# Two token blocks of a gated MoE layer through seven of eight block products, with transposes moved to TensorE

## The chip, the cores and the metric

The program runs on one core of a Trainium2 chip. The metric is the device time of one execution in microseconds (us), the median over the runs shown. The profile is one execution, recorded by the hardware profiler. Engines: TensorE (PE, with its weight loads as PEld), VectorE (DVE), ScalarE (ACT), GpSimd (POOL) and SyncE (SP, which here only issues DMAs).

## What is computed

Three layers in a row, all in fp32 at the interface:

```
h    = x @ omega.T - |x|^2/2 ; phi(x) = exp(h - max(h)) / sqrt(128)        (x = q or k, scaled)
attn = phi(q) @ (phi(k).T @ v) / (phi(q) @ sum(phi(k)) + 1e-6)             4 x 8 heads, 576 x 64
y    = (sigmoid(attn @ w_gate) * (attn @ w_val)) @ w_out                   2304 tokens, 512 -> 1536 -> 512
out  = soft mixture of 8 experts over y (dispatch and combine softmax, 4 slots each, 512 -> 1024 -> 512)
```

## The kernel before, in words

The 32 heads are handled as 16 attention units of two heads (`step_chunks`, L701). A unit's numerators (`chunk_num`, L658) yield a piece of x, the MoE input with features on partitions; x is split into a rounded part (hi) and a rest (lo), and stays in SBUF as tile `XT` of its block (`xt`, L696). The 2304 tokens are five blocks: four of 512 and one of 256 (`BLOCKS`, L27).

The MoE layer runs in 60 steps (`STEPS`, L33), a step being one block j and one slice f of 128 of the 1536 hidden features. A step has a gate product (`gate`, L828), a value product (`val`, L839) and an output product (`down`, L853). Each is four products of 128x128 weights, and each of those three TensorE passes (`three`, L452: hi times hi, hi times lo, lo times hi), so 12 instructions. In blocks 0 to 3 they are 128x512, in block 4 128x256. The weights come from DRAM scratch `wscr` (`load_w`, L750) and are split into hi and lo for every step (`split_w`, L798: hi on ACT or DVE, lo on POOL or DVE). The gate's sigmoid is made of Abs, Exp, Ln and Exp on ACT with one DVE instruction between, so that ACT keeps one activation table for the whole program.

The blocks stand in this order (`GROUPS`, L32): block 0's first six slices, block 1, block 0's rest, blocks 2, 3 and 4. Attention units 0 to 7 go with the first group, 8 to 11 with block 1, 12 to 15 with block 2. For units 10 and later (`N_SPLIT`, L58) the phi(q) tiles are transposed not on TensorE but by 32x32 DVE transposes and a round trip through DRAM (`turn_q`, L642: eight DVE transposes, 2 DMAs out and 8 in for a unit). The last layer's logits, transposes and slot sums follow each block (`moe2_chunks`, L967); its weights w1 are loaded through ACT's queue (`load_w1`, L984) into tiles that have come free (`EXTAGS`, L973), w2 through SP's queue.

What order each engine gets is settled when the program is built: every instruction is recorded with a due time (from `SPAN`, L75, and the job list at the end of `body`) and the engines that may run it, and `schedule` (L240) lists them by due time, dependence and a table of costs (`cost`, L200). On the chip each engine runs its list in order, and waits only on semaphores. PSUM has eight banks: `ga` and `va` for the gate and value products, `o0` to `o3` for the output sums, two of `fl` for everything else.

Of the kernel before, what the change touches and what calls it, by code (L numbers as in the profile page):

```python
# [34 lines left out]
ENDS = {i for i, (j, f) in enumerate(STEPS) if (j, f) in {(j, e - 1) for j, _, e in GROUPS}}  # L35
DONE = [1, 0, 2, 3, 4]
# [21 lines left out]
N_SPLIT = 10  # L58
N_NUM = 10
LATE8 = 0.3  # L60
# [14 lines left out]
SPAN = [88.0, 115.0, 60.0, 120.0, 105.0, 45.0]  # L75
# [11 lines left out]
HOP = 0.16  # L87
TURN = 0.2
# [15 lines left out]
class Plan:  # L104
# [135 lines left out]
    def schedule(self):  # L240
# [46 lines left out]
        dma = 0.0  # L287
        order = []
# [60 lines left out]
        while ev:  # L349
# [13 lines left out]
            for e in E:  # L363
                while free_at[e] <= now + 1e-9:
# [21 lines left out]
                    c, held = self.cost(e, alt[1], alt[3], outs, ins)  # L386
                    if held:
                        port = now + c
# [31 lines left out]
def body(ctx, tc, nc, qkT, tok, von, omT, wall, phi, w1, w2, ident_d, srep_d, rrep_d, mask_d, out):  # L420
# [31 lines left out]
    def three(ps, lhs, rhs, first=True, last=True):  # L452
        (lh, ll), (rh, rl) = lhs, rhs
        PE.matmul(ps, lh, rh, start=first, stop=False)
        PE.matmul(ps, lh, rl, start=False, stop=False)
        PE.matmul(ps, ll, rh, start=False, stop=last)
# [86 lines left out]
    def prep_qk(u, kind):  # L543
# [3 lines left out]
        if u == N_SPLIT and kind == 0:  # L547
            split_regions()
# [109 lines left out]
    def chunk_num(u, half):  # L658
# [13 lines left out]
        else:  # L672
# [77 lines left out]
    def load_w(i):  # L750
# [47 lines left out]
    def split_w(i, part):  # L798
        if i >= NB * NF:
            return  # L800
        end = (i, part) == (NB * NF - 1, 2)
# [5 lines left out]
        if (i, part) == (LAST - 1, 2):  # L807
            load_part(5)
# [613 lines left out]
```

## Time and profile before

| | |
|---|---|
| median of 3 runs | 677.5 us (676.54 to 678.06) |
| span of the profiled execution | 676.7 us; the page gives no time beyond it |
| TensorE busy, instructions | 652.3 us, 4292 |
| VectorE busy | 446.8 us |
| ScalarE busy | 430.3 us |
| GpSimd busy | 276.9 us |
| DMA moved | 144.78 MB, mean 214 GB/s |

Busy time counts the union of an engine's instructions; matmuls overlap each other, so that one lasts longer than the distance from its start to the next one's. A row of the timeline merges instructions of one kind: start, time from the first start to the last end, engine, line, instruction, output and inputs by tile name, sizes, count, and in brackets how long the engine was idle before and what ended that.

### The profile page before, as it was taken

How to read it: one execution, taken by the hardware profiler on the slowest of the kernel's cores; microseconds unless marked ns; L12 is line 12 of the kernel's file. 1: busy time of each engine (PE TensorE's matmuls, PEld its weight loads, DVE VectorE, ACT ScalarE, POOL GpSimd, SP SyncE). 2: the span in 40 equal slices, each digit the busy share in tenths (PEclk: the TensorE clock that was granted, in tenths of full speed). 3: DMA queues.
4: the chain of work that ended last, by engine and by line, in shares of the span. 5: the costliest groups of instructions: out<-in, count | busy, mean ns of one | idle time of the engine just before them, and what ended most of it. 6: DMA issues, size and time to landing. Idle time of an engine off the chain costs nothing. (4 is left out here: it accounts for less than half of the span.)

```text
span 676.7 us, 12729 instructions
## 1 busy us (share of the span) xinstructions
PE 652.3 (96%) x4292; PEld 521.2 (77%) x4292; DVE 446.8 (66%) x1399; ACT 430.3 (64%) x971; POOL 276.9 (41%) x240
## 2 busy tenths in 40 slices
PE   7898999999999999899999999999999999999994
PEld 5675777768788888788788888777888789889663
DVE  4888989889987474766686666556543337666322
ACT  5898989889787575767567666546344445664011
POOL 0546335454455344445344444343544444342100
PEclk9999999999999999999999999999999999999998
DMA  7887857677875337575557424579963339767997
GB/s 256 294 268 235 286 187 261 216 235 264 294 235 191 89 124 222 182 201 161 164 166 227 133 67 136 166 234 349 257 223 93 99 104 312 220 226 256 352 348 221
DMA packets 64241, 144.78 MB, mean 214 GB/s; under 512 B 7600, under 2 KB 21680, under 8 KB 64176
## 3 DMA queue, kind: packets, MB, share of 16 engines
q1 hardware_dynamic: 58352, 126.60, 58.2%
q10 hardware_dynamic: 5824, 17.37, 7.7%
q8 instruction: 34, 0.56, 0.3%
q14 instruction: 31, 0.25, 0.1%
HBM read 122.44 MB, written 17.30 MB: 206 GB/s over the span
## 5 line engine op out<-in xcount | busy, mean ns | idle before, releaser
L413 POOL TENSOR_TENSOR w<-ws,w 128x512 fp32r<-128x512 f32 x139 | 181.4, 1307 | 247.4 <-ACT w L413 88.4
L413 PE MATMUL ga<-XT,w 128*128 128x512 f32 (+1 forms) x720 | 170.3, 377 | 2.3 <-POOL XT L413 1.2
L413 PE MATMUL va<-XT,w 128*128 128x512 f32 (+1 forms) x720 | 167.4, 375 | 0.9 <-DVE ga_a L413 0.6
L413 PE MATMUL o<-gt,w 128*128 128x512 f32 (+1 forms) x720 | 166.6, 374 | 0.9 <-POOL w L413 0.9
L413 PEld LDWEIGHTS ga<-XT,w 128*128 128x128 f32 x720 | 123.7, 188 | 29.8 <-issue 3.5
L413 PEld LDWEIGHTS o<-gt,w 128*128 128x128 f32 x720 | 124.8, 188 | 26.1 <-issue 2.2
L413 PEld LDWEIGHTS va<-XT,w 128*128 128x128 f32 x720 | 123.8, 189 | 27.3 <-issue 3.2
L413 ACT ACTIVATE w<-ws 128x512 fp32r<-128x512 f32 x110 | 69.1, 628 | 59.6 <-POOL w L413 17.2
L413 ACT ACTIVATE g<-g 128x128 f32<-128x128 f32 (+5 forms) x213 | 78.2, 420 | 23.2 <-DVE g L413 12.3
L413 PE MATMUL fl<-g,g 64*128 64x128 f32 (+4 forms) x686 | 83.1, 313 | 3.6 <-ACT g L413 1.7
L413 PEld LDWEIGHTS fl<-g,g 64*128 64x128 f32 (+2 forms) x686 | 59.8, 182 | 24.3 <-issue 9.0
L413 ACT ACTIVATE ga_a<-ga_a 128x512 f32<-128x512 f32 (+1 forms) x120 | 69.8, 582 | 12.8 <-DVE ga_a L413 10.9
L413 ACT ACTIVATE ga_a<-ga 128x512 f32<-128x512 f32 (+1 forms) x60 | 33.1, 552 | 63.4 <-PE ga L413 63.0
L413 DVE SCALAR_TENSOR_TENSOR ga_a<-ga,ga_a 128x512 f32<-128x512 f32 (+1 forms) x60 | 38.0, 633 | 36.9 <-ACT ga_a L413 36.0
L413 DVE CAST w<-ws 128x512 fp32r<-128x512 f32 x52 | 22.5, 432 | 52.9 <-PE ga L413 34.7
L413 DVE TENSOR_TENSOR ga_a<-va,ga_a 128x512 f32<-128x512 f32 (+1 forms) x60 | 38.0, 634 | 24.2 <-ACT ga_a L413 16.7
L413 ACT ACTIVATE x2T<-g 128x512 f32<-128x512 f32 x72 | 46.0, 664 | 5.1 <-DVE x L413 3.0
L413 ACT ACTIVATE g1b<-g1b,g 128x128 f32<-128x128 f32 x128 | 41.1, 390 | 7.1 <-DVE g L413 7.1
L413 ACT ACTIVATE ga_a<-ga_a,one_b 128x512 f32<-128x512 f32 (+1 forms) x60 | 40.6, 677 | 1.2
L413 DVE CUSTOM_DVE_ANT_0 g<-fl,g 128x128 f32<-128x128 f32 x142 | 32.4, 286 | 9.0 <-PE fl L413 8.7
L413 DVE TENSOR_SCALAR x2T<-x2T 128x512 f32<-128x512 f32 (+1 forms) x72 | 35.9, 515 | 2.0 <-ACT x2T L413 1.8
L413 POOL TENSOR_TENSOR g<-g 128x640 f32<-128x640 f32 (+1 forms) x18 | 22.2, 1231 | 34.2 <-DMA g<-in_tok 24.7
(202 smaller groups left out, 773.6 us busy)
## 6 DMA issues: line engine op xcount, KB each, us to landing
ws<-wscr SPq DMA_DIRECT2D x42, 512.0 KB, 3.8
ws<-wscr SPq DMA_DIRECT2D x78, 256.0 KB, 3.2
g<-in_wall SPq DMA_DIRECT2D x36, 512.0 KB, 5.0
wscr<-x SPq DMA_DIRECT2D x36, 256.0 KB, 4.6
g<-in_qkT SPq DMA_DIRECT2D x15, 576.0 KB, 4.8
g<-in_tok SPq DMA_DIRECT2D x15, 576.0 KB, 4.9
g<-in_w ACTq DMA_DIRECT2D x16, 512.0 KB, 5.5
XT<-in_w ACTq DMA_DIRECT2D x12, 512.0 KB, 5.5
```

Source lines behind the costliest of these rows:

```text
L413: ins = getattr(self.eng[e], method)(*a, **k)
```

## The change

Blocks 2 and 3 leave `STEPS` and become a pair. For two slices f and f+1 at once, the gate stage (and the value stage) of the pair is a product of 2x2 blocks: 256 hidden features by 512 inputs, by 512 inputs times 1024 tokens. It is now computed by seven block products in place of eight (Strassen's scheme in the form with 15 sums). A block product is six TensorE instructions of 128x512 (`product` in `pair_up`). The sums of tokens are made once (`pair_tokens`), those of weights for each pair of slices and each of the two stages (`pair_split`), and those of results at each evacuation (`pair_up`). All eight attention units 8 to 15 now stand beside block 1 and the rest of block 0. `chunk_num` writes x of blocks 2 and 3 unsplit in fp32 (`xq`). The output products of block 2 follow each pair of slices, those of block 3 come in a stage of their own after it, from gated values kept in SBUF (`GB`); w_out is split once for each of the two. In the pair and in block 4 the gate is one Sigmoid, whose activation table has to be loaded, and Exp's again where Exp follows. `N_SPLIT` of 16 leaves all transposes on TensorE. The w1 loads have other tiles and due times (`EXTAGS`).

```diff
-GROUPS = [(0, 0, CUT), (1, 0, NF), (0, CUT, NF), (2, 0, NF), (3, 0, NF), (4, 0, NF)]
+GROUPS = [(0, 0, CUT), (1, 0, NF), (0, CUT, NF), (4, 0, NF)]
+PAIR = (2, 3)
-N_SPLIT = 10
+N_SPLIT = 16
...
-SPAN = [88.0, 115.0, 60.0, 120.0, 105.0, 45.0]
+SPAN = [88.0, 143.0, 71.0, 45.0]
+SPANQ = 147.0
+SPAND = 33.0
...
         a = T([128, 512], "ga_a", F32, 2)[:, 0:n]
+        if i >= LAST:
+            ACT.activation(out=a, in_=ps, func=AF.Sigmoid)
+            return a
...
+    def pair_tokens():
+
+        a, b = (xq(j) for j in PAIR)
+        b11, b21, b12, b22 = a[:, 0:2], a[:, 2:4], b[:, 0:2], b[:, 2:4]
...
+        for k, r in zip((6, 5, 7, 3, 4, 2, 1), regs):
+            OT[k] = r
+        sum_of(t1, b12, b11, ALU.subtract)
+        hi_lo(OT[1], b11)
+        hi_lo(OT[5], t1)
+        hi_lo(OT[2], b21)
+        sum_of(t2, b22, t1, ALU.subtract, ("DVE",))
+        hi_lo(OT[6], t2, ("DVE",))
+        sum_of(t3, b22, b12, ALU.subtract, ("DVE",))
+        hi_lo(OT[7], t3)
+        sum_of(b21, b21, t2, ALU.subtract)
+        hi_lo(OT[4], b21)
+        hi_lo(OT[3], b22)
...
+    def pair_split(part):
+
+        x, y = WR[:, 2 * part, :], WR[:, 2 * part + 1, :]
+        a11, a12, a21, a22 = x[:, 0:256], x[:, 256:512], y[:, 0:256], y[:, 256:512]
+        s1, s2 = SG[7][:, 0:256], SG[7][:, 256:512]
+        sum_of(s1, a21, a22, ALU.add)
+        sum_of(s2, s1, a11, ALU.subtract)
+        hi_lo(OW[6], s2)
+        hi_lo(OW[1], a11)
+        sum_of(a21, a11, a21, ALU.subtract)
+        hi_lo(OW[7], a21)
+        hi_lo(OW[5], s1)
+        sum_of(s2, a12, s2, ALU.subtract)
+        hi_lo(OW[2], a12)
+        hi_lo(OW[4], a22)
+        hi_lo(OW[3], s2)
+
+    def pair_up(f, part, t0, dt):
+
+        b1 = bank("ga")
+        b2, b3 = (bank(x) for x in (("va", "fl") if part == 0 else ("fl", "va")))
+        def product(m, ps, n, first=True):
+            plan.t = t0 + dt * n / 7
+            w, x = OW[m], OT[m]
+            for k in range(2):
+                r = slice(128 * k, 128 * k + 128)
+                three(ps, (w[:, 0, r], w[:, 1, r]), (x[:, 0, k], x[:, 1, k]), first and k == 0, k == 1, not first)
...
+        product(6, b2, 0)
+        ACT.activation(out=u, in_=b2, func=AF.Copy)
+        product(1, b1, 1)
+        DVE.tensor_tensor(out=u, in0=b1, in1=u, op=ALU.add)
+        product(7, b3, 2)
+        DVE.tensor_tensor(out=v, in0=b3, in1=u, op=ALU.add)
+        product(5, b2, 3)
+        DVE.tensor_tensor(out=v, in0=b2, in1=v, op=ALU.add)
+        done(v, SG[3], f + 1)
+        product(2, b1, 4, first=False)
+        done(b1, SG[0], SG[0])
+        product(4, b3, 5, first=False)
+        DVE.tensor_tensor(out=c, in0=b3, in1=u, op=ALU.add)
+        done(c, SG[2], SG[2])
+        product(3, b2, 6, first=False)
+        DVE.tensor_tensor(out=u, in0=b2, in1=u, op=ALU.add)
+        done(u, SG[1], f)
...
+        def late_split(f):
+            gt = T([128, 2, 512], "gt", F32R, 2)
+            hi_of(gt[:, 0], GB[f], SITE["hg"])
+            lo_of(gt[:, 1], GB[f], gt[:, 0], SITE["lg"])
+            G["b", f] = gt
...
-    EXTAGS = ["XT", "g0", "g1", "g2", "g3", "g4", "XT", "XT"]
+    EXTAGS = ["XT", "XT", "g2", "g3", "g4", "XT", "g0", "g1"]
...
-                         1: (range(8, 12), start + LATE8 * span, start + span + 0.9 * SPAN[2]),
-                         3: (range(12, 16), start, start + 0.92 * span)}.get(g, ((), 0, 0))
+                         1: (range(8, 16), start + LATE8 * span, start + span + SPAN[2] - READY - EARLY)}.get(g, ((), 0, 0))
```

Where the instructions now stand, at three places. TensorE in the middle of blocks 2 and 3: before, one step of block 3 (gate, value, output).

```order
L413 MATMUL ga_645<-XT_461,w0_639 128x512 x12
L413 MATMUL va_648<-XT_461,w1_643 128x512 x12
L413 MATMUL o0_602<-gt_642,w2_644 128x512 x3
L413 MATMUL o1_603<-gt_642,w2_644 128x512 x3
L413 MATMUL o2_604<-gt_642,w2_644 128x512 x3
L413 MATMUL o3_605<-gt_642,w2_644 128x512 x3
```

Now, the value stage of one pair of slices and the start of the output products of block 2 (`g2`, `g3`, `g4`, `g1b` hold the token operands, `w0`, `w1`, `more` the weight operands).

```order
L425 MATMUL fl_558<-g2_489,w0_498 128x512 x6
L425 MATMUL ga_557<-g1b_492,w0_498 128x512 x6
L425 MATMUL va_559<-g3_490,w1_499 128x512 x6
L425 MATMUL fl_558<-g2_489,w1_499 128x512 x6
L425 MATMUL ga_557<-g4_491,more_500 128x512 x6
L425 MATMUL va_559<-g4_491,more_500 128x512 x6
L425 MATMUL fl_558<-g3_490,more_500 128x512 x6
L425 MATMUL o0_525<-gt_560,w2_556 128x512
L425 MATMUL o1_526<-gt_560,w2_556 128x512
L425 MATMUL o2_527<-gt_560,w2_556 128x512
L425 MATMUL o0_525<-gt_560,w2_556 128x512 x2
L425 MATMUL o1_526<-gt_560,w2_556 128x512 x2
```

Runs of 12 on one bank, with nothing of theirs evacuated in between, have become runs of six: banks `fl`, `ga` and `va` come again two products later, in part on top of the sum that stands there.

VectorE where the last attention unit ends: before, its numerators and the split of x into `XT`.

```order
L413 TENSOR_TENSOR gt_581<-ga_a_578,gt_581 128x512
L413 TENSOR_TENSOR g4_84<-fl_572,g4_84 64x288
L413 TENSOR_TENSOR g4_84<-fl_573,g4_84 64x288
L413 TENSOR_TENSOR XT_461<-g4_84,XT_461 128x288
L413 TENSOR_TENSOR g4_84<-fl_575,g4_84 64x288
L413 TENSOR_TENSOR g4_84<-fl_576,g4_84 64x288
L413 CAST XT_461<-g4_84 128x224
L413 CAST w0_586<-ws_85 128x512
L413 CAST w1_589<-ws_85 128x512
L413 TENSOR_TENSOR w1_589<-ws_85,w1_589 128x512
```

Now, numerators into the unsplit x (`XT_282`), then the token sums (into `XT_488`) and the rests of the operands (`g2_489`, `g3_490`).

```order
L425 TENSOR_TENSOR ga_a_477<-va_483,ga_a_477 128x512
L425 CAST gt_484<-ga_a_477 128x512
L425 TENSOR_TENSOR XT_282<-fl_481,g4_84 64x224
L425 TENSOR_TENSOR g4_84<-fl_481,g4_84 64x64
L425 TENSOR_TENSOR XT_282<-fl_482,g4_84 64x224
L425 TENSOR_TENSOR g4_84<-fl_482,g4_84 64x64
L425 TENSOR_TENSOR XT_488<-XT_282,XT_488 128x1024
L425 TENSOR_TENSOR XT_488<-XT_282 128x1024
L425 COPY acc_71<-fl_487 128x512
L425 TENSOR_TENSOR g2_489<-XT_488,g2_489 128x1024
L425 TENSOR_TENSOR g3_490<-XT_488,g3_490 128x1024
L425 TENSOR_TENSOR g3_490<-XT_282,g3_490 128x1024
```

What moved: all units end ahead of blocks 2 and 3, and sums and splits of 128x1024 stand between the last numerators and the first block products.

ScalarE in block 4: before, one step's gate among the weight splits.

```order
L413 ACTIVATE ga_a_724<-ga_723 128x256
L413 ACTIVATE w0_725<-ws_85 128x512
L413 ACTIVATE ga_a_724<-ga_a_724 128x256
L413 ACTIVATE cs_721<-cs_721 128x128
L413 ACTIVATE ga_a_724<-ga_a_724,one_b_64 128x256
L413 ACTIVATE w1_727<-ws_85 128x512
L413 ACTIVATE ga_a_724<-ga_a_724 128x256
L413 ACTIVATE w2_728<-ws_85 128x512
```

Now, three gates (`ga_a`), with the Exps of the last layer (`lt`, `mx2`, `cs`) between them.

```order
L425 ACTIVATE ga_a_663<-ga_662 128x256
L425 ACT_TABLE_LOAD
L425 ACTIVATE lt_649,mx2_650<-fl_648,mx2_650 128x128
L425 ACTIVATE mx2_650<-mrun_72,mx2_650 128x1
L425 ACTIVATE w2_668<-ws_85 128x512
L425 ACT_TABLE_LOAD
L425 ACTIVATE ga_a_674<-ga_673 128x256
L425 ACTIVATE w1_677<-ws_85 128x512
L425 ACT_TABLE_LOAD
L425 ACTIVATE cs_671<-cs_671 128x128
L425 DMA g1a_645<-in_w1 128x1024
L425 ACT_TABLE_LOAD
```

Four instructions of a gate have become one, and each change between Sigmoid and Exp carries a table load; there are 13 in the program in place of 1.

## Rows read from the trace of the kernel before

**Rows 1.** The page's first part: span, and busy time of each engine.
```profile
span 676.7 us, 12729 instructions
PE 652.3 (96%) x4292; PEld 521.2 (77%) x4292; DVE 446.8 (66%) x1399; ACT 430.3 (64%) x971; POOL 276.9 (41%) x240
```

**Rows 2.** Windows: stretch, length, busy us (instructions) by engine, clock, DMA share, GB/s.
```profile
141.70:332.40 190.70, 188.53 (x1017) 151.73 (x1015) 136.60 (x389) 137.11 (x296) 89.46 (x76) 1.00 0.61 193
332.40:559.50 227.10, 226.15 (x1171) 184.72 (x1170) 129.34 (x368) 126.50 (x255) 99.26 (x83) 1.00 0.57 175
559.50:621.00 61.50, 58.90 (x488) 55.70 (x486) 41.36 (x103) 36.59 (x82) 24.57 (x19) 1.00 0.77 243
```

**Rows 3.** Timeline of TensorE in block 3, nothing between the products.
```profile
517.50 2.88 PE L413 MATMUL ga<-XT,w 128*128 128x512 f32 x12
520.22 2.88 PE L413 MATMUL va<-XT,w 128*128 128x512 f32 x12
```

**Rows 4.** Timeline of TensorE where an early unit's transposes stand among gate products.
```profile
113.53 0.60 PE L413 MATMUL fl<-ident,g 128*128 128x128 f32 x4
113.89 0.71 PE L413 MATMUL ga<-XT,w 128*128 128x512 f32 x2
114.43 0.60 PE L413 MATMUL fl<-ident,g 128*128 128x128 f32 x4
```

**Rows 5.** Groups by form: count | busy us, mean ns of one | idle us before.
```profile
L413 PE MATMUL fl<-ident,g 128*128 128x128 f32 x58 | 9.9, 272 | 0.0
L413 DVE TENSOR_TENSOR ga_a<-va,ga_a 128x512 f32<-128x512 f32 x48 | 33.0, 687 | 21.2 <-ACT ga_a L413 13.7 <-PE va L413 6.7 <-ACT g L413 0.5
L413 DVE TENSOR_TENSOR gt<-ga_a,gt 128x256 fp32r<-128x256 f32 x12 | 5.0, 418 | 0.1
L413 ACT ACTIVATE ga_a<-ga_a 128x512 f32<-128x512 f32 x96 | 60.0, 625 | 8.7 <-DVE ga_a L413 6.9 <-DMA g<-in_w 0.8
L413 ACT ACTIVATE ga_a<-ga_a 128x256 f32<-128x256 f32 x24 | 9.8, 409 | 4.0 <-DVE ga_a L413 4.0
L413 POOL TENSOR_TENSOR w<-ws,w 128x512 fp32r<-128x512 f32 x139 | 181.4, 1307 | 247.4 <-ACT w L413 88.4 <-DVE w L413 59.6 <-DVE g L413 20.6
L413 POOL TENSOR_TENSOR XT<-g,XT 128x224 fp32r<-128x224 f32 x12 | 8.0, 665 | 6.2 <-DVE XT L413 2.6 <-DVE x L413 1.6 <-DVE x2T L413 1.0
```

**Rows 6.** Timeline of TensorE's waits for numerators of units 10 and later, and DVE ahead.
```profile
272.37 0.43 DVE L413 CAST g<-g 128x512 fp32r<-128x512 f32 x1 [3.67 <-DMA g<-qscr]
274.90 0.63 PE L413 MATMUL fl<-g 128*128 128x288 f32 x3 [1.15 <-DVE g L413]
276.20 0.67 PE L413 MATMUL fl<-g 128*128 128x288 f32 x3 [0.68 <-DVE g L413]
455.11 0.63 PE L413 MATMUL fl<-g 128*128 128x288 f32 x3 [0.68 <-DVE g L413]
```

**Rows 7.** Timeline of DVE and POOL at the same moment.
```profile
221.47 1.28 POOL L413 TENSOR_TENSOR w<-ws,w 128x512 fp32r<-128x512 f32 x1 [2.83 <-DVE w L413]
222.02 1.02 DVE L413 CAST gt<-ga_a 128x512 fp32r<-128x512 f32 x1
```

**Rows 8.** Timeline of TensorE's waits in block 4.
```profile
578.30 1.70 PE L413 MATMUL va<-XT,w 128*128 128x256 f32 x12 [0.60 <-DVE ga_a L413]
591.20 1.69 PE L413 MATMUL ga<-XT,w 128*128 128x256 f32 x12 [0.81 <-DVE ga_a L413]
595.55 1.46 PE L413 MATMUL o<-gt,w 128*128 128x256 f32 x10 [0.91 <-POOL w L413]
```

**Rows 9.** Timeline of ScalarE: the one table load, and the end of block 4.
```profile
0.73 1.28 ACT L413 ACT_TABLE_LOAD   x1 [0.73 <-PEq L1417]
624.28 0.60 ACT L413 ACTIVATE x<-fl 128x512 f32<-128x512 f32 x1 [0.30 <-PE fl L413]
625.65 0.26 ACT L413 ACTIVATE dt<-dt 128x64 f32<-128x64 f32 x1 [0.77 <-DVE dt L413]
```

More of the change, by code (lines that the diff above doesn't have):

```diff
@@ L287, in schedule @@
         dma = 0.0
+        table = 0
         order = []
@@ L386, in schedule @@
                     c, held = self.cost(e, alt[1], alt[3], outs, ins)
+                    want = {AF.Exp: 0, AF.Ln: 0, AF.Sigmoid: 1}.get(alt[3].get("func"), table) if e == "ACT" else table
+                    if want != table:
+                        c, table = c + RELOAD, want
                     if held:
@@ L450, in warm, with three @@
             PE.matmul(ps, x[:, 0:128], x, start=True, stop=True)
[L452 removed]
+    def three(ps, lhs, rhs, first=True, last=True, onto=False):
         (lh, ll), (rh, rl) = lhs, rhs
[L454 to L456 removed]
+        PE.matmul(ps, lh, rh, start=first, stop=False, skip_group_check=onto)
+        PE.matmul(ps, lh, rl, start=False, stop=False, skip_group_check=onto)
+        PE.matmul(ps, ll, rh, start=False, stop=last, skip_group_check=onto)
     def stream(name, t):
@@ L546, in prep_qk @@
             return
[L547 removed]
+        if u == N_NUM and kind == 0:
             split_regions()
@@ L699, in xt, with xq @@
         return XT[j]
+    XQ = {}
+    def xq(b):
+        if not XQ:
+            t = T([128, 2, 4, 512], "XT", F32, 3)
+            XQ.update({j: t[:, k] for k, j in enumerate(PAIR)})
+        return XQ[b]
     def step_chunks(u):
@@ new lines, in body, with hi_lo, sum_of @@
+    OT, OW, SG, GB = {}, {}, [], []
+    def hi_lo(dst, src, lo=("POOL", "DVE")):
+        hi_of(dst[:, 0], src, ("ACT", "DVE"))
+        lo_of(dst[:, 1], src, dst[:, 0], lo)
+    def sum_of(dst, a, b, op, eng=("DVE", "POOL")):
+        plan.add([(e, "tensor_tensor", (), dict(out=dst, in0=a, in1=b, op=op)) for e in eng])
+    def pair_tokens():
+        a, b = (xq(j) for j in PAIR)
+        b11, b21, b12, b22 = a[:, 0:2], a[:, 2:4], b[:, 0:2], b[:, 2:4]
+        t = T([128, 8, 512], "XT", F32, 3)
+        SG.extend(t[:, k] for k in range(8))
+        t1, t2, t3 = (t[:, 2 * k:2 * k + 2] for k in range(3))
+        regs = [carve(g, at, [2, 2, 512]) for g in [region(k, F32R) for k in (2, 3, 4)] for at in (0, 2048)]
+        regs.append(carve(half_region(1, F32R), 0, [2, 2, 512]))
+        for k, r in zip((6, 5, 7, 3, 4, 2, 1), regs):
[11 more added lines that the diff above has]
+        hi_lo(OT[3], b22)
@@ new lines, in pair_tiles, with pair_load @@
+    def pair_tiles():
+        for k, tag in ((0, "w0"), (2, "w1")):
+            t = T([128, 2, 2, 256], tag, F32R)
+            OW.update({m: t[:, n] for n, m in enumerate(((6, 1), (7, 5))[k // 2])})
+        t = T([128, 4, 2, 256], "more", F32R)
+        OW.update({m: t[:, n] for n, m in enumerate((2, 4, 3))})
+    def pair_load(f, part, at):
+        SP.dma_start(out=WR[:, at:at + 2, :], in_=wscr[f:f + 2, :, part, :].rearrange("f q c -> q f c"))
+    def pair_split(part):
[13 more added lines that the diff above has]
+        hi_lo(OW[3], s2)
@@ new lines, in pair_up, with done @@
+    def pair_up(f, part, t0, dt):
+        b1 = bank("ga")
+        b2, b3 = (bank(x) for x in (("va", "fl") if part == 0 else ("fl", "va")))
+        u, v, c = (SG[1], SG[3], SG[2]) if part == 0 else SG[4:7]
+        def product(m, ps, n, first=True):
[4 more added lines that the diff above has]
+                three(ps, (w[:, 0, r], w[:, 1, r]), (x[:, 0, k], x[:, 1, k]), first and k == 0, k == 1, not first)
+        def done(x, s, to):
+            if part == 0:
+                ACT.activation(out=s, in_=x, func=AF.Sigmoid)
+                return
+            psum = x.space == PSUM
+            if isinstance(to, int):
+                to = GB[to]
+            sum_of(to, x, s, ALU.mult, ("DVE",) if psum else ("DVE", "POOL"))
+            if to is s:
+                gt = T([128, 2, 512], "gt", F32R, 2)
+                hi_of(gt[:, 0], s, SITE["hg"])
+                lo_of(gt[:, 1], s, gt[:, 0], SITE["lg"])
+                G["a", f + (s is SG[2])] = gt
+        product(6, b2, 0)
[15 more added lines that the diff above has]
+        done(u, SG[1], f)
@@ L861, in body, with split_out @@
+    def split_out(f, at):
+        if f % 2:
+            w = [T([128, 512], "ga_a", F32R, 2) for _ in range(2)]
+        else:
+            t = T([128, 2, 512], "w2", F32R)
+            w = [t[:, 0], t[:, 1]]
+        raw = WR[:, at + f % 2, :]
+        hi_of(w[0], raw, SITE["hw"])
+        lo_of(w[1], raw, w[0], SITE["lw"])
+        WS["out", f] = w
     ms = {}
```

132 lines of the change are left out of this document (100 added, 32 removed).

## The prediction

> **What bounds the kernel now.** I read the busy times first, then the stretches, then the timeline. TensorE is busy 652.3 of 676.7 us [rows 1], but matmuls overlap, so the share alone does not say that it is full. The stretches do: from 141.7 to 332.4 and from 332.4 to 559.5 it stands still for 2.2 and 1.0 us, while DVE and ACT are busy 72% of the first and 56 to 57% of the second, and the clock is 1.00 throughout [rows 2]. So there the time is TensorE's work, and what an instruction costs is its distance to the next one. Twelve of 128x512 take from 517.50 to 520.22, 2.72 us [rows 3], so one is worth **0.227 us**, not the 0.38 that it lasts. An fp32 transpose of 128x128 lasts 272 ns [rows 5], but from 113.53 to 113.89 four of them pass in 0.36 us, and the next two gate products with the pipe's tail take 0.54 to 114.43, 0.09 more than twice 0.227 [rows 4]: 0.45 for four, **0.11 us** each.
>
> **The sum, part by part.**
>
> 1. *Block products, minus 16.3.* Before, the gate and value products of blocks 2 and 3 are 24 steps of 24 instructions, 576 of 128x512. Now 6 pairs of slices, 2 stages, 7 products of 6: 504. 72 x 0.227 = 16.3 us less, all on the engine that has no idle time. The output products stay: 288.
>
> 2. *Transposes, plus 5.3.* Units 10 to 15 put 8 transposes each on TensorE, 48 x 0.11 = 5.3 us. What they replace (8 DVE transposes and 10 DMAs a unit) lies beside TensorE's work, except for what it makes TensorE wait. The bounds are 0.09 and 0.272 a piece; I take 0.11, as measured among gate products.
>  The Trainium skill, page "TensorE: Matmul & The Clock Gate", section "Part 4: PE-mode transpose", gives a transpose about 275 ns in a kernel. The 272 ns that one lasts agree, the spacing of 0.11 does not; by 275 ns this term would be 13.2 and the sum 7.9 higher (an estimate; as a rival, below).
>
> 3. *Waits for numerators, minus 1.5.* TensorE waited 1.15, 0.68 and 0.68 us for DVE at numerators of units 10 and later, DVE standing behind the DMA of the round trip [rows 6]. That is 2.5 at most. The short way over PSUM still has a split into hi and lo, so I leave 1.0. If it waits more than now, this term is as much as +1.
>
> 4. *Into the pair, plus 2.0.* After the last numerators DVE has four multiplies of at most 224 columns (some 0.9, from 0.418 for 256), then two sums and three rests of 128x1024. A 128x512 takes 0.687 [rows 5], so one is about 1.4 and the chain 7.8 us. TensorE has 48 instructions of block 0 left as cover, 10.9 us. But DVE and POOL do not get at SBUF together: a CAST that began at 222.02 ended 0.29 after POOL's instruction did, and took 1.02 [rows 7]. Two POOL instructions of 128x1024 (2 x 1.307 each) in the way make the chain 13.0, which is 2.1 late; the sums of products 2 to 4 come behind it. Between 0 and 4; I take 2.0, the case with both in the way.
>
> 5. *Inside the pair, plus 1.5.* TensorE has 504 + 144 instructions, 147 us. From the order I count for these: DVE 66 sums out of PSUM, 18 of 128x512 and 9 splits at 0.687 and 57 of 128x256 at 0.418, 88 us; ACT 82 of 128x256 at 0.409 and 58 of 128x512 at 0.625, 70 us; POOL 75 of 128x256 (0.665 for 224 columns, so 0.76) and 14 at 1.307, 75 us. That is 60, 47 and 51% of 147, little more than in the same blocks before, so I cost all this at nothing. What isn't covered is the hand-over of banks: in each of 12 stages four products go into a bank that DVE or ACT must have read first, with two products, 2.72 us, between. The matmul's tail is 0.16, the sum 0.69, so 1.9 us are spare. A late one costs what exceeds 1.9, and DVE loses about 0.6 when it meets a POOL instruction (a CAST of 1.02 where one of that size takes 0.43) [rows 6, 7]. So one meeting never shows, three in a row cost a little. Bounds 0 and 5; I take 1.5, 0.12 a stage.
>
> 6. *Output products of block 3 on their own, plus 1.0.* 144 x 0.227 = 32.6 us, work that was there before. For each slice (2.72 us) w_out and the gated value are split anew: POOL 1.307, DVE 0.43 and 0.69 [rows 5, 6], which together hold the SBUF port 2.4 of 2.72. That is tight, but it is two slices ahead. Bounds 0 and 7 (0.6 a slice); I take 1.0. DMA: some 19 loads of w1, 6 of w_out and block 2's turns are 14.6 MB in 38 us, 384 GB/s, where block 4's stretch ran at 243 GB/s with a share of 0.77 [rows 2], 316 at full share. So w1 comes some 8 us late, but its first use is 50 us off.
>
> 7. *Block 4, minus 1.0.* Its waits for the gate were 0.60 and 0.81 [rows 8]. One Sigmoid in place of four ACT and one DVE instruction makes that chain shorter. Four table loads stand among the gates; at 1.28 us [rows 9], two of them and the Exps between end about when the next gate is due, since each product of 12 takes some 1.5 [rows 8], and value and output leave 3 us between two gates. The wait of 0.91 for a split behind a late weight load [rows 8] stays. Between -1.7 and +3, the latter if the backlog of w1 delays two weight loads.
>
> 8. *The end, plus 0.6.* The table of Exp has to come back after the copy that ends at 624.88, and before the Exp at 625.65, for which ACT had been free 0.77 [rows 9]: 1.28 - 0.77 = 0.5, and 0.1 for the last gate.
>  The Trainium skill, page "ScalarE: Activation LUTs", section "What ACT_TABLE_LOAD costs", counts a switch as 1.28 and a drain of 1.38, and would have functions grouped by table. The trace shows the 1.28 and no run here shows the drain; with it this term would be about 2, and the sum 1.4 higher.
>
> The sum is -16.3 + 5.3 - 1.5 + 2.0 + 1.5 + 1.0 - 1.0 + 0.6 = **-8.4 us**. The profiled execution has 676.7, so 668.3; the median of the runs shown, 677.5, lies 0.8 above it, so **669** for a median.
>
> **The rivals.**
>
> *A, no new waits.* Terms 4 to 6 at nothing and term 3 whole: -16.3 + 5.3 - 2.5 - 1.0 + 0.6 = -13.9, about 664. For it: TensorE waited hardly 1 us in 227 before [rows 2]. Against it: nothing of that stretch had to be evacuated before two products later.
>
> *B, slower: the hand-over of banks becomes the bound.* Place: the 48 hand-overs inside the pair. The other terms without term 5 make -9.9, so it decides from 0.2 us lost at each on average, that is 2.1 us of delay behind an evacuation. Where each loses 0.35, it is +16.8, and 684. For it: the chain is four engines long (a sum waits for the copy, the next sum for that one), in order, and DVE has to pass POOL. Against it: DVE is busy only 60%.
>
> *C, transposes at their full length.* If each of the 48 holds TensorE for the 0.272 that it lasts, 7.8 more: 677, no change. The spacing of 0.11 speaks against it [rows 4]. [...]
>
> *D, the shared port.* Terms 4 to 6 near their upper bounds, 4 + 3 + 5 in place of 4.5: 676.5. For it: 2.4 of 2.72 us in term 6, and sums of 128x1024 in a place that DVE and POOL both need.
>
> That the change does not take work off TensorE is no case: the order has 72 fewer of 128x512 and 48 more transposes.
>
> **How the numbers follow.** Forecast 0.60 (664.5 to 673), A 0.11, B 0.11, C 0.05, D 0.13. A measurement of this kernel can tell about 0.2% from no change, 1.35 us: 676.1 to 678.9 is the same. Faster: the forecast, A and three quarters of D, 0.81. Same: C and most of the rest of D, 0.07. Slower: B and a remainder, 0.12. The range leaves out B and half of A: 664 to 677.
>
> **What would show it.** Right: 128x512 products of TensorE 1656 in place of 1728, 0.227 us apart inside the pair; the pair from its first block product to block 4 in 186 to 191 us (147 + 32.7, the last 12 of block 0, 3 for the last layer, the waits); no qscr DMAs; 12 more table loads of 1.28 with no gap of TensorE behind them; one wait of 1 to 4 us at the first block products. Wrong: gaps of TensorE before the 6-runs that start on `fl`, `ga` or `va` again, with DVE as releaser, over 10 us in all (B); transposes over 0.2 us apart (C); waits for POOL in the output stage of block 3 (D).

## The result, and the profile after

The changed kernel takes **667.9 us** (median of 4 runs, 666.81 to 671.05) against 677.0 us for the kernel before in the same comparison (674.37 to 678.06): ratio 0.988, interval 0.9847 to 0.9913. The prediction was 669, faster. The profiled execution of the changed kernel is the one of 666.81; its span is 664.9 us, 11.8 below the span before, while the medians differ by 9.2. Single executions of this kernel scatter by 4 us, so terms of the sum are compared below by stretches of the trace and not by totals. The profiled one is the fastest of the four; its mean granted clock is 0.997, that of the others 0.990 to 0.995, so stages that wait may be longer in them.

The first part of the page of the changed kernel, beside [rows 1]:

```profile
span 664.9 us, 12634 instructions
PE 644.0 (97%) x4268; PEld 513.2 (77%) x4268; DVE 479.7 (72%) x1379; ACT 410.6 (62%) x937; POOL 289.2 (43%) x272
```

Windows of the changed kernel: block 1 with the rest of block 0 and all eight units, the pair (from the first block product to block 4), block 4, the end. The columns are those of [rows 2].

```profile
140.40:357.30 216.90, 216.90 (x1282) 177.97 (x1281) 167.22 (x521) 170.14 (x387) 103.62 (x87) 1.00 0.50 157
357.30:547.70 190.40, 188.90 (x879) 149.87 (x877) 130.57 (x229) 79.89 (x163) 94.49 (x102) 1.00 0.48 152
547.70:611.40 63.70, 61.18 (x502) 57.45 (x498) 42.93 (x92) 30.11 (x50) 27.58 (x21) 1.00 0.80 261
611.40:664.90 53.50, 45.07 (x816) 30.81 (x815) 17.68 (x60) 8.89 (x27) 1.90 (x2) 0.97 0.89 316
```

The two long stretches took 190.7 + 227.1 = 417.8 us before [rows 2] and take 216.9 + 190.4 = 407.3 now: **10.5 us less**. TensorE is busy 8.9 us less in them (414.7 to 405.8) and still 1.6 us less (3.1 to 1.5). Block 4 took 63.1 (559.5 to the first of the last logits, below) and takes 63.7, the end took 54.1 and takes 53.5. The remaining 1.3 us had been won by 140, and already at 93, in a stretch whose order is the same in both kernels up to about 95 us; so they need not come from the change. TensorE's timeline before, then now:

```profile
622.59 1.07 PE L413 MATMUL ga<-x2T,phs 128*32 128x128 f32 x16
```

```profile
611.43 1.07 PE L425 MATMUL ga<-x2T,phs 128*32 128x128 f32 x16
```

TensorE's timeline, its waits of over 0.19 us from the pair's beginning through block 4:

```profile
359.51 1.66 PE L425 MATMUL va<-g,w 128*128 128x512 f32 x6 [0.20 <-DVE ga_a L425]
361.93 0.47 PE L425 MATMUL o<-gt,w 128*128 128x512 f32 x1 [0.76 <-ACT XT L425]
...
538.41 2.56 PE L425 MATMUL o<-gt,w 128*128 128x512 f32 x10 [0.46 <-DVE w L425]
...
573.07 1.22 PE L425 MATMUL o<-gt,w 128*128 128x256 f32 x8 [0.73 <-POOL w L425]
576.79 0.50 PE L425 MATMUL va<-XT,w 128*128 128x256 f32 x2 [1.06 <-DVE ga_a L425]
577.81 1.44 PE L425 MATMUL va<-XT,w 128*128 128x256 f32 x10 [0.51 <-POOL w L425]
584.38 1.46 PE L425 MATMUL o<-gt,w 128*128 128x256 f32 x10 [0.21 <-POOL w L425]
```

Entering the pair costs 0.96 us. Then nothing until the output stage of block 3, with 0.46, and four waits in block 4, 2.5 us, about as many as before, but now behind weight loads: VectorE and ScalarE stood still for a weight load there (its timeline and ScalarE's, below), VectorE ahead of the multiply by the gate that TensorE waited for at 576.79.

```profile
575.98 0.43 DVE L425 CAST w<-ws 128x512 fp32r<-128x512 f32 x1 [2.26 <-DMA ws<-wscr]
...
577.40 0.63 ACT L425 ACTIVATE w<-ws 128x512 fp32r<-128x512 f32 x1 [5.91 <-DMA ws<-wscr]
```

The hand-over of a bank in a value stage, timeline of the changed kernel (TensorE's first, ScalarE's copy, TensorE's next on the same bank `fl`):

```profile
449.11 1.52 PE L425 MATMUL fl<-g,w 128*128 128x512 f32 x6
450.67 0.60 ACT L425 ACTIVATE XT<-fl 128x512 f32<-128x512 f32 x1
453.19 1.07 PE L425 MATMUL fl<-g,w 128*128 128x512 f32 x4
```

The copy ends at 451.27, the bank is written again at 453.19: 1.92 us spare, the 1.9 of the prediction. And the beat of the stages, TensorE's timeline at the second product (its bank `ga`, operand `g1b`), once in each stage (the one between is left out):

```profile
450.47 1.52 PE L425 MATMUL ga<-g1b,w 128*128 128x512 f32 x6
...
475.26 1.52 PE L425 MATMUL ga<-g1b,w 128*128 128x512 f32 x6
```

A value stage and a gate stage with the 24 output products of a pair of slices come to **24.79 us** (450.47 to 475.26). TensorE's own work in them is 108 instructions of 0.227, 24.5. Most of the other 0.3 stands in the three products of each stage whose weights lie in `more` (TensorE's timeline):

```profile
454.55 1.56 PE L425 MATMUL ga<-g,more 128*128 128x512 f32 x6
455.95 1.57 PE L425 MATMUL va<-g,more 128*128 128x512 f32 x6
457.36 1.57 PE L425 MATMUL fl<-g,more 128*128 128x512 f32 x6
458.76 2.93 PE L425 MATMUL o<-gt,w 128*128 128x512 f32 x12
```

Six of them take 1.40 us where six others take 1.36. Over the whole pair these 216 instructions follow each other at a median of 0.234 us and the other 288 block-product instructions at 0.227, without a wait: 0.13 us a stage, some 1.6 us for the 12 stages. Why is not shown. The beat is the measure in most experiments below.

### The profile page after: what moved, and what is told of

Its sections match the earlier page's. It is cut to its first block, busy times and chain, and to the rows that moved or that the text cites. A ratio compares the mean times of both kernels' runs of the same rounds, so it can differ in the third digit from the quotient of the medians.

```text
span 664.9 us, 12634 instructions
## 1 busy us (share of the span) xinstructions
PE 644.0 (97%) x4268; PEld 513.2 (77%) x4268; DVE 479.7 (72%) x1379; ACT 410.6 (62%) x937; POOL 289.2 (43%) x272
## 4 chain that ended last, share of the span: by engine, by line
PE 84%; DMA 5%; DVE 4%; ACT 2%; POOL 1%; SPq 1%; issue 1%; DVEq 0%; POOLq 0%; ACTq 0%
PE o L425 24%; PE fl L425 23%; PE va L425 19%; PE ga L425 18%; DMA g<-in_tok 2%; DMA x2T<-x 1%; DMA g<-in_w 1%; DVE g L425 1%; DMA ws<-wscr 1%; SPq L425 1%; DVE XT L425 1%; POOL g L425 1%; DVE ga_a L425 1%; ACT w L425 0%; DMA g<-in_qkT 0%
## 5 line engine op out<-in xcount | busy, mean ns | idle before, releaser
L425 POOL TENSOR_TENSOR w<-ws,w 128x512 fp32r<-128x512 f32 (+1 forms) x101 | 120.6, 1195 | 161.3 <-ACT w L425 67.2
L425 PE MATMUL o<-gt,w 128*128 128x512 f32 (+1 forms) x576 | 134.7, 372 | 2.2 <-POOL w L425 0.9
L425 PE MATMUL ga<-XT,w 128*128 128x512 f32 (+1 forms) x432 | 101.6, 367 | 0.9 <-POOL XT L425 0.9
L425 ACT ACTIVATE w<-ws 128x512 fp32r<-128x512 f32 (+1 forms) x100 | 57.7, 579 | 72.3 <-PE o L425 28.1
L425 PE MATMUL va<-XT,w 128*128 128x512 f32 (+1 forms) x432 | 100.1, 366 | 1.6 <-DVE ga_a L425 1.1
L425 ACT ACTIVATE g<-g 128x128 f32<-128x128 f32 (+4 forms) x206 | 73.8, 414 | 16.9 <-DVE g L425 12.9
L425 PEld LDWEIGHTS ga<-XT,w 128*128 128x128 f32 x432 | 69.9, 189 | 16.8 <-issue 4.7
L425 PEld LDWEIGHTS va<-XT,w 128*128 128x128 f32 x432 | 70.5, 189 | 15.2 <-issue 2.4
L425 PE MATMUL o<-gt,ga_a 128*128 128x512 f32 x144 | 35.4, 393 | 0.0
L425 ACT ACTIVATE ga_a<-ga_a 128x512 f32<-128x512 f32 x48 | 30.0, 624 | 1.7 <-DVE ga_a L425 1.4
```

The lines of the kernel that those rows point to most:

```text
L425: ins = getattr(self.eng[e], method)(*a, **k)
```

## The experiments

Beside each ratio to the kernel before stands what it makes against the changed kernel: (ratio - 0.988) times the median before of that comparison. Both ratios have intervals of 0.2 to 0.4 per cent either way, so such a difference is known to some 3 us.

**1. Eight products again.**

```diff
+            if m == 6:
+                for k in range(2):
+                    r = slice(128 * k, 128 * k + 128)
+                    three(ps, (w[:, 0, r], w[:, 1, r]), (x[:, 0, k], x[:, 1, k]), k == 0, k == 1)
```

> The first block product of each stage is issued twice (the second time into a bank started afresh), so that the values are unchanged and 72 TensorE instructions of 128x512 come back: as many as eight products would have. Theory (TensorE's instructions are the time inside the pair, 0.227 us each): +16.3 us over the changed kernel, 684 us, with the pair 190 + 16 = 206 us long. Rival (the hand-over of banks or the vector engines set the pace there, TensorE has hidden slack): the second passing takes up slack, under +8 us, below 676.

Measured: 686.3 us, ratio 1.0149 (1.0107 to 1.0191), 18.2 us over the changed kernel. TensorE's timeline:

```profile
448.16 1.52 PE L425 MATMUL ga<-g1b,w 128*128 128x512 f32 x6
...
475.68 1.52 PE L425 MATMUL ga<-g1b,w 128*128 128x512 f32 x6
```

The beat is 27.52, 2.73 more: 12 instructions of 0.227 are 2.72. So a block product costs what its instructions cost, and no slack took it up. Another 2.3 us stand in the output stage of block 3, which took 48.8 us in place of 46.5, though nothing of it was meant to change; experiments 9 to 12 are about that. Here and below this stage is taken from the last instruction on operand `g1b` to block 4, so the last five block products, some 7 us, are in it.

**2. Each transpose twice**, in units 8 to 15.

```diff
+            for again in range(2 if u >= 8 else 1):
```

> Units 8 to 15 make each of their 10 transposes on TensorE twice into the same place: 80 more transposes, values unchanged. Theory (a transpose costs its distance to the next, 0.11 us): +8.8 us over the changed kernel, 676.7. Rival C (it holds TensorE for the 0.272 us that it lasts): +21.8, 689.6. Third (in that stretch vector work sets the time, not TensorE): about 0, 668.

Measured: 676.8 us, ratio 1.0012 (0.9984 to 1.0041), 8.9 us over the changed kernel, where 8.8 were expected at 0.11 us. In the profile block 1 with the rest of block 0 takes 224.9 us (139.9 to 364.8) against 216.9, 8.0 for the 80 transposes, 0.10 each. The output stage of block 3 is 3.8 us longer in the same execution, so that the total meets 8.8 partly by luck; the stretch is the better measure. Rival C falls.

**3. The round trip through DRAM for units 10 to 15 again.**

```diff
-N_SPLIT = 16
+N_SPLIT = 10
```

> Undoes the transposes alone: units 10 to 15 go through DVE transposes and DRAM again, all else as changed. Theory (terms 2 and 3 of the prediction): 48 transposes less are 5.3 us less of TensorE, waits for numerators as before, 1.5 to 2.5 us: 2.8 to 3.8 us faster than the changed kernel, 664 to 665. Rival (DVE is 77 per cent busy there now that eight units stand beside block 1, so the 48 DVE transposes and the round trips cost waits that are longer than before): the same or up to 5 us slower, 668 to 673.

Measured: 711.8 us, ratio 1.0525 (1.049 to 1.056), **43.6 us** over the changed kernel. Both theories miss it by far. Two windows of this kernel, columns as above, and the timeline of DVE and of TensorE there:

```profile
355.00:375.00 20.00, 7.52 (x30) 5.85 (x31) 6.07 (x32) 5.10 (x11) 0.37 (x2) 0.50 0.37 101
390.00:410.00 20.00, 11.63 (x32) 6.65 (x33) 12.17 (x22) 7.70 (x14) 5.18 (x4) 0.50 0.26 63
```

```profile
355.94 0.43 DVE L425 CAST g<-g 128x512 fp32r<-128x512 f32 x1 [2.52 <-DMA g<-qscr]
...
356.52 1.56 PE L425 MATMUL fl<-g 128*128 128x288 f32 x3 [5.44 <-DVE g L425]
365.03 1.09 PE L425 MATMUL fl<-g 128*128 128x288 f32 x3 [6.95 <-DVE g L425]
```

The last units are not done when block 0 runs out of products, and the pair needs them: its first product begins at 387.67, 30.3 us later than in the changed kernel, and numerators still stand among its products until 400. Now the round trips stand bare. TensorE waits 5.44 and 6.95 us for DVE, which waits for `qscr` the first time, and the second time for a split of ScalarE's that had waited 10.94 us for `qscr`; some 14 shorter waits follow. The granted clock, 1.00 until 340, is 0.50 (1.2 GHz) behind these waits, in the windows from 355 to 375 and from 390 to 410. Before the change the same round trips cost 2.5 us at most [rows 6], with products of the next blocks beside them. So the short way over TensorE is not a term of +5.3 that could be spared; with all units ahead of the pair and these due times it is a condition. Part of the 43.6 may belong to the due times: between the DMA out to `qscr` at 354.53 and those back at 359.59 SyncE's list has seven `x2T` DMAs, 4.47 us. No run tries the round trip with due times of its own.

**4. The gate by Abs, Exp, Ln and Exp again**, in the pair and in block 4.

```diff
...
-                ACT.activation(out=s, in_=x, func=AF.Sigmoid)
...
+                ACT.activation(out=y, in_=x, func=AF.Abs)
+                ACT.activation(out=y, in_=y, func=AF.Exp, scale=-1.0)
+                ACT.activation(out=y, in_=y, func=AF.Ln, bias=one_b)
+                DVE.scalar_tensor_tensor(out=y, in0=x, scalar=0.0, in1=y, op0=ALU.min, op1=ALU.subtract)
+                ACT.activation(out=s, in_=y, func=AF.Exp)
```

> Undoes the Sigmoid alone: in the pair and in block 4 each gate is Abs, Exp, Ln and Exp on ScalarE with one VectorE instruction again, one table load in the program. Theory (vector work is covered inside the pair): 72 more ACT instructions of 0.625 us and 24 of DVE of 0.69 make ACT 66 and DVE 77 per cent busy there, no wait of TensorE over 2 us in all; block 4 and the end together by terms 7 and 8 about +0.4: 667 to 671. Rival (ACT and DVE stand in the chain of hand-overs, so that longer gates delay evacuations): 0.4 us or more at each of 12 gate stages and the value stages behind them, +5 to +15, 673 to 683.

Measured: 678.6 us, ratio 1.0028 (1.0007 to 1.0049), 10.0 us over the changed kernel, as much as the whole gain. The theory, that this work is covered, falls. TensorE's timeline:

```profile
441.59 1.52 PE L425 MATMUL ga<-g1b,w 128*128 128x512 f32 x6
...
467.82 1.52 PE L425 MATMUL ga<-g1b,w 128*128 128x512 f32 x6
```

Here the beat is 26.23, 1.44 more, with DVE busy 118.7 and ACT 93.9 of the 148.6 us of the product stages; it is 25.1 in the last ones. By stretches: 4.7 us more from the first to the last product stage, 5.8 in the output stage of block 3, 1.4 in block 4, and 0.5 less at the end, where no table has to come back (65.1 and 53.0 us for the last two). That the longer gates delay evacuations fits the pair's 4.7, but the plan moved work too: in the product stages 16 weight splits that ScalarE had are now VectorE's. The 5.8 stand where there is no gate at all, in the stage that grew in every kernel tried. So what can be put down to the gate itself is at most about 6 us, not 10.

**5. Two thirds of each block product.**

```diff
-                three(ps, (w[:, 0, r], w[:, 1, r]), (x[:, 0, k], x[:, 1, k]), first and k == 0, k == 1, not first)
+                PE.matmul(ps, w[:, 0, r], x[:, 0, k], start=first and k == 0, stop=False, skip_group_check=not first)
+                PE.matmul(ps, w[:, 0, r], x[:, 1, k], start=False, stop=k == 1, skip_group_check=not first)
```

> Leaves out the third pass (rest of the weights times rounded tokens) of every block product in the pair: 4 instructions instead of 6, 168 of 128x512 less; the output is less exact, evacuations and splits stay. It asks how far the cover of the vector engines reaches. If TensorE still sets the pace: 168 x 0.227 = 38.1 us less than the changed kernel, 629 to 630. Theory (term 5: DVE is busy 97 of the 144 us from the first to the last product stage; in 106 us it would be 92 per cent, and a bank comes again after 1.82 us with 0.85 for tail and sum): most of it, 25 to 36 us, 632 to 643, with waits for DVE in the pair. Rival B (the hand-over of banks is already near its limit): under 15 us, above 653.

Measured: 644.3 us, ratio 0.9538 (0.951 to 0.9565), 23.1 us under the changed kernel, just outside the theory's 25 to 36 and far from the rival's 15. TensorE's timeline:

```profile
426.76 1.07 PE L425 MATMUL ga<-g1b,w 128*128 128x512 f32 x4
...
445.49 1.07 PE L425 MATMUL ga<-g1b,w 128*128 128x512 f32 x4
```

Where the beat is steady it is 18.73: 6.06 less of the 28 x 0.227 = 6.36 taken out. So even with DVE busy 98.6 of 115.9 us the steady stages are TensorE's. From the first to the last product stage it is 28.0 less; part of what is missing lies in the pair's first 40 us (waits of 1.2 and 1.8 us), and 4.2 us in the output stage of block 3, which is 50.7 us long although its five block products have become shorter, and 2.7 in block 4, 66.4 us.

**6 and 7. The first product's bank held longer**, by four and by six copies in place of one.

```diff
-        ACT.activation(out=u, in_=b2, func=AF.Copy)
+        for _ in range(4):
+            ACT.activation(out=u, in_=b2, func=AF.Copy)
```

> The bank of the first product of each of the 12 stages is read four times by ScalarE instead of once (the same copy, values unchanged), so that it comes free some 1.8 us later, and the sums behind the copy too. Theory (term 5: a bank comes again after 2.72 us, 1.9 us of it spare): no wait for it, 0 to 2 us over the changed kernel, 668 to 670. Rival B (nothing is spare, DVE's chain behind the copy is what counts): 1 us and more at each of the 12 stages, 680 and above.

> The same with six copies, so that the bank is read for some 3.7 us. Theory: spare time is 1.9 us, the bank comes 3.7 + 0.2 - 2.72 = 1.1 to 1.2 us late at each of 12 stages, unless output products of block 2 stand between: 10 to 14 us over the changed kernel, 678 to 682. If it costs as little as four copies do, more is spare than the prediction counted. Rival B: twice and a half the cost of four copies, over 20 us.

Measured: 676.5 us, ratio 1.0006 (0.9985 to 1.0028), and 683.6, ratio 1.0114 (1.0088 to 1.0139): 8.5 and 15.8 us over the changed kernel. TensorE's timeline with four copies, a pair of slices:

```profile
441.46 1.52 PE L425 MATMUL ga<-g1b,w 128*128 128x512 f32 x6
466.75 1.52 PE L425 MATMUL ga<-g1b,w 128*128 128x512 f32 x6
```

and with six:

```profile
432.14 1.52 PE L425 MATMUL ga<-g1b,w 128*128 128x512 f32 x6
458.18 1.52 PE L425 MATMUL ga<-g1b,w 128*128 128x512 f32 x6
```

The beats are 25.29 and 26.04, 0.50 and 1.25 more for two stages. The first is a little over what the theory allowed (2 us in all; six times 0.50 are 3), the second half of the 2.2 to 2.4 expected for two stages. In the steady pairs each kernel has one wait a pair, in the value stage, where the first product's bank is written again (TensorE's timeline, four copies, then six):

```profile
482.19 1.66 PE L425 MATMUL fl<-g,w 128*128 128x512 f32 x6 [0.19 <-ACT XT L425]
```

```profile
461.55 2.93 PE L425 MATMUL fl<-g,w 128*128 128x512 f32 x10 [0.49 <-ACT w L425]
```

In the gate stage 12 output products stand between the first product and the next one on its bank, so nothing is lost there, and 1.25 is the price of one stage, beside the 1.1 to 1.2 expected for one. So the spare time is of the size predicted, and rival B's 1 us at each stage is not seen. But the totals rose by more than the beats, and missed the theory: the output stage of block 3 took 53.8 and 52.6 us.

**8 to 12. The output stage of block 3, and block 4's weights.** In experiment 6 that stage waited 2.77 us; timeline of ScalarE, TensorE and SyncE's queue in it:

```profile
537.14 3.39 SPq L425 DMA_DIRECT2D x2T<-x  x5
540.63 4.20 SPq L425 DMA_DIRECT2D ws<-wscr  x2
544.41 0.63 ACT L425 ACTIVATE w<-ws 128x512 fp32r<-128x512 f32 x1 [7.54 <-DMA ws<-wscr]
545.61 0.73 PE L425 MATMUL o<-gt,w 128*128 128x512 f32 x2 [2.77 <-ACT w L425]
```

TensorE waits for a split, the split for a load of w_out, and ahead of such loads SyncE's list has the DMAs that turn block 2's output (`x2T`), 11.8 us for 16 of them in this stretch. Yet in the changed kernel, too, the same 16 hold that queue, for 12.6 us, and the stage waits only 0.46; so the holding alone does not decide. Experiment 8 came first, on block 4, where the same DMAs of block 3 stand among the weight loads; 9 to 12 ask the question for the output stage. Their edits in turn: the early Exp and every second `x2T` DMA of block 3 on ScalarE's queue; four copies with block 2's `x2T` DMAs on ScalarE's queue; four copies with the due times of w1 moved; the changed kernel with both sets of DMAs moved and the early Exp; four copies with w1 held back to block 4.

```diff
+            if i == NS - 1:
+                ACT.activation(out=z, in_=one_b, func=AF.Exp)
...
-            jobs += [(start - SPAND + 1.0 + 8 * k, "ex", load_w1) for k in range(4)]
+            jobs += [(start + 4.0 + 5 * k, "ex", load_w1) for k in range(4)]
...
+            q = ACT if j == PAIR[0] or j == PAIR[1] and i % 2 else SP
-            SP.dma_start(out=x[32 * h:32 * h + 32, 512 * i:512 * i + 512], in_=y[32 * i:32 * i + 32, h])
+            q.dma_start(out=x[32 * h:32 * h + 32, 512 * i:512 * i + 512], in_=y[32 * i:32 * i + 32, h])
...
+            plan.floor = 532.0 if e > 1 else 0.0
             for c in range(4):
                 ACT.dma_start(out=W1[e][c], in_=w1[e, :, 1024 * c:1024 * c + 1024])
```

> A trial of a better version: a one-element Exp behind the last Sigmoid brings Exp's table back while ScalarE is idle, and every second DMA of block 3's turned output goes through ScalarE's queue, so that block 4's weight loads stand behind fewer of them on SyncE's. Theory: 0.4 us at the end and up to 2.3 us of block 4's waits for weights: 665 to 667.5. Rival (the loads are late because the DMA engines are full, not because their issue is late): 0.4 us at most, 667.5 to 669, with the waits for split weights in block 4 as long as now.

Measured: 666.7 us, ratio 0.9875 (0.9854 to 0.9897): no difference from the changed kernel that these runs can tell. The early Exp missed its place, the plan listed it ahead of the last Sigmoid, and the table still comes back behind the copy. Block 4's waits of over 0.17 us fell from 2.5 to 0.7 (TensorE's timeline):

```profile
568.07 1.45 PE L425 MATMUL va<-XT,w 128*128 128x256 f32 x10 [0.52 <-POOL w L425]
581.16 0.50 PE L425 MATMUL o<-gt,w 128*128 128x256 f32 x2 [0.18 <-ACT w L425]
```

and block 4 to 61.9 us from 63.7, at a DMA share of 0.78 against 0.80. That fits loads that were late because they were issued late. It is not shown: experiment 11, with the same DMAs of block 3 moved, has waits of 1.1 us in block 4, fewer too, but block 4 takes 63.5 us, and in experiment 6, where they stay on SyncE's queue, 63.0. The start and the output stage, 0.8 us longer each, took the gain back in the profiled execution.

> The kernel with four copies of the first product's bank again, and in it the 16 DMAs of block 2's turned output go through ScalarE's queue instead of SyncE's. It asks why the output stage of block 3 (from the last first product to block 4) took 53.8 us there against 46.5 in the changed kernel, with w_out landing late. Theory S (the w_out loads stand in SyncE's list behind these DMAs, each of which holds the queue 0.6 to 1.2 us): the stage falls to 46 to 48 us, the whole to 668 to 671. Rival W (the DMA engines are full of w1 and w2): 52 to 55, the time stays at 676.

> The kernel with four copies again, with the six w1 loads that start in the output stage of block 3 put off into block 4 and behind it, all else alike. Theory S: the DMAs of the turned output still stand ahead of the w_out loads, the stage keeps over 50 us. Rival W: without w1 on the DMA engines the stage falls to 46 to 48 us. In both, the tail gets longer, since w1 lands later; what is read is this one stage.

> The run before this one did not move w1: its loads have a due time only, ScalarE's list issued them as early as before (its queue carried 8.4 MB between 504 and 552 us in both kernels). Here the six late w1 loads get an earliest time in the plan as well, so that in ScalarE's list they stand behind the last split of w_out, at block 4; the first product's bank is still copied four times. Theory S (w_out waits in SyncE's list behind the DMAs of the turned output, whatever else is moved): the output stage of block 3 keeps over 50 us (53.8 and 52.8 in the two kernels with four copies). Rival W (the DMA engines are full of w1, and both the turned output and w_out land late for it): it falls to 46 to 48 us. In both, some 12.6 MB come 45 us later, of which block 4 can take 20 per cent of its time: the end 15 to 30 us later, 690 to 705.

Measured: 675.8 us (ratio 0.998, 0.9952 to 1.0009), 678.6 (one run), and 705.1 (ratio 1.0432, 1.0398 to 1.0465). Experiment 10 says nothing on w1, which the edit didn't move; it repeats that the stage is long with four copies, 52.8 us. Windows of the stage, from experiments 6, 9 and 12:

```profile
505.50:559.30 53.80, 49.46 (x232) 37.71 (x230) 33.62 (x62) 12.31 (x22) 17.04 (x13) 0.94 0.87 282
```

```profile
502.90:550.60 47.70, 46.69 (x231) 35.45 (x229) 33.73 (x61) 13.11 (x23) 17.58 (x13) 1.00 0.96 307
```

```profile
506.30:556.30 50.00, 47.91 (x232) 36.90 (x230) 30.28 (x57) 15.84 (x28) 15.33 (x12) 0.97 0.41 116
```

With the turns on ScalarE's queue the stage falls to 47.7 us though the DMA engines are at 0.96 (theory S, in the profile). But that execution is the fastest of ten, 671.3 us; the median, 675.8, is not the 668 to 671 that was expected, and not different from experiment 6's 676.5. Without w1 and a share of 0.41 it is 50.0, between both theories, and TensorE still waits 1.22 us for a split of w_out.

> The changed kernel with the early Exp, block 2's turned output through ScalarE's queue, and every second DMA of block 3's. Theory S: the output stage of block 3 at 46 to 46.5 us (nothing to gain over its 0.5 us of waits), block 4 as in the run with the early Exp: 664.5 to 667. Rival: the DMAs on ScalarE's list stand behind DVE's transposes and delay its splits of weights, 668 to 672.

Measured: 672.8 us, ratio 0.993 (0.9903 to 0.9956), 3.4 over the changed kernel, hardly more than its uncertainty: nearer the rival. The output stage is 48.2 us, with a wait of 1.27 for the same kind of split (TensorE's timeline):

```profile
542.06 0.73 PE L425 MATMUL o<-gt,ga_a 128*128 128x512 f32 x2 [1.27 <-ACT ga_a L425]
```

So moving the turns did not better the good case, and that it mends the bad one is seen in one execution and not in the medians. In all these kernels the longest waits of the stage stand behind late loads of w_out; whether SyncE's list or the DMA engines make them late, these runs do not settle. Apart from experiment 5, which leaves out a third of the block products' passes, no kernel was measurably faster than the changed one.

## Why the prediction was right

Its sum was -8.4 us, and -9.2 came by the medians, with an interval (0.33 per cent either way) that is wider than the 0.2 per cent it had counted on. Of its signs, 128x512 products of TensorE are 1656, `qscr` is gone, there are 12 table loads more, and the pair took 190.4 us, in its 186 to 191. By steps:

1. *Block products, -16.3.* Right: instructions of 0.227 us, but 0.234 in the 216 whose weights lie in `more`; shown by the beat of experiment 1 (2.73 for 12) and from the other side by experiment 5 (6.06 of 6.36).
2. *Transposes, +5.3.* Right: 0.10 by stretches; the 0.11 by totals is partly luck (experiment 2). The Trainium skill, page "TensorE: Matmul & The Clock Gate", section "Part 4: PE-mode transpose", has about 275 ns for one (of bf16) in a kernel; as a duration the trace agrees [rows 5], as a price it does not.
 Steps 1 and 2 come to -11.0; busy time in the two stretches fell by 8.9. Of the other 2.1, some 1.6 stand in the products with `more`; the rest was not followed to single instructions.
3. *Waits for numerators, -1.5.* They are gone altogether, -2.5 [rows 6], the far end of its range. What the prediction left out is the other side: had the round trip stayed, with these due times, its cost would not have been these 2.5 but some 44 (experiment 3).
4. *Into the pair, +2.0.* 0.96, its place as named. (The profile puts the 0.76 down to ScalarE's copy, which ended at 361.80; VectorE's CAST into `gt`, behind a token sum of 2.07 us, ended at 361.78.)
5. *Inside the pair, +1.5.* No wait shows behind the entry. The 1.9 us spare were right (1.92 in the timeline, and experiments 6 and 7), though in the steady pairs the first hand-over is tight in the value stage alone, and the 0.12 a stage set aside for meetings of DVE and POOL were not needed for them. That the slower products with `more` cost nearly the same, 0.13 a stage, is luck. Rival B falls for this kernel. But "I cost all this at nothing" holds only because the gate had become one instruction: with the four, and the splits that moved to VectorE with them, it costs 4.7 us from the first to the last product stage (experiment 4). The prediction counted 58 to 82 instructions of ACT and never asked what the Sigmoid itself was worth.
6. *Output products of block 3, +1.0.* 0.46, from two causes together: a weight load that came late, and the shared port that the prediction named. Timeline of ScalarE, POOL, VectorE and TensorE ahead of that wait:

```profile
535.80 1.15 ACT L425 ACTIVATE w<-ws 128x512 fp32r<-128x512 f32 x2 [1.56 <-DMA ws<-wscr]
536.51 1.30 POOL L425 TENSOR_TENSOR w<-ws,w 128x512 fp32r<-128x512 f32 x1 [2.02 <-ACT w L425]
536.98 1.37 DVE L425 TENSOR_TENSOR w<-ws,w 128x512 fp32r<-128x512 f32 x1 [0.89 <-ACT w L425]
537.34 0.61 PE L425 MATMUL o<-gt,w 128*128 128x512 f32 x2
```

 VectorE's instruction ended 0.54 behind POOL's and took 1.37 us in place of 0.69; with 0.69 it would have ended at 537.67, before TensorE was free at 537.95. The same stage was 0.8 to 7.3 us longer in every kernel tried, with waits behind late loads of w_out; that was the part of the change with the least margin, and term 6 dealt with DMA by the late w1 alone.
7. *Block 4, -1.0.* Mis-sized, with the wrong sign: +0.6 (63.1 to 63.7). The waits for the gate went, and waits for weights of 2.3 us came, between 572 and 578. Where from is open: with half of block 3's turns off SyncE's list block 4 took 61.9 in experiment 8 and 63.5 in experiment 11. The step fails in "the wait of 0.91 for a split behind a late weight load stays".
8. *The end, +0.6.* Right in mechanism. Timeline of ScalarE:

```profile
613.12 0.60 ACT L425 ACTIVATE x<-fl 128x512 f32<-128x512 f32 x1 [0.30 <-PE fl L425]
613.74 1.28 ACT L425 ACT_TABLE_LOAD   x1
615.03 0.26 ACT L425 ACTIVATE dt<-dt 128x64 f32<-128x64 f32 x1
```

The Exp starts 1.31 us behind the copy in place of 0.77 [rows 9]. From the first product of the last logits to the next layer's first it is 6.57 us (611.43 to 618.00) after 6.15: +0.4. The Trainium skill's page "ScalarE: Activation LUTs", section "What ACT_TABLE_LOAD costs", adds a drain of 1.38 to the 1.28; here the load begins 0.02 behind the copy and the Exp 0.01 behind the load, no drain shows.

Terms 4 to 6 were 4.5 and measured 1.4, term 3 was 1.0 short, both towards faster; busy time (2.1, the products with `more` in it) and term 7 (1.6) lay the other way. So the 669 is near for its two large terms, and in the small ones because errors of both signs met. The start and the end gave 1.3 and 1.0 more, for which no step stood, and which a repeat need not show.

## What to carry to other kernels

Price TensorE's work by the distance between starts in a stretch without gaps, and trust it to a few per cent. What that price needs is cover, and cover belongs to the arrangement: ask of each part of a change what happens without it, as the short transposes (44 us with these due times) and the one-instruction gate (at most 6 of 10 us) were conditions of a gain that the block products alone seemed to make. Look for the stage with the least margin in the queues that issue DMAs too, not only in the engines' busy shares.

## What was not expected of the hardware

The granted clock followed short waits of TensorE: in experiment 3 it stood at 0.50 in both windows above, in the first of which TensorE was busy 7.5 of 20 us, and in experiment 6 waits of 2.77 and 1.26 us within 5 us left a mean of 0.94 over the 53.8 us of the stage, where the changed kernel, with one wait of 0.46, kept 1.00. Part of what such a wait costs is thus paid behind it: of the 7.3 us that this stage is longer, 3.5 are busy time of TensorE (49.46 us for 232 instructions, 45.96 for 231 in the changed kernel). And 16 DMAs of 64 KB, 1 MB in all, held SyncE's queue for 11.8 us in that stage, so that loads listed behind them were issued later.
